# Two-headed attention and gated MLP on one core: a second copy of one head's queries and keys, and a later start of DMA transposes

## The chip, the cores and the metric

The kernel runs on one core of a Trainium2 chip. A core has a matmul engine (TensorE, here PE, with PEld for its weight loads), a vector engine (DVE), a scalar engine (ACT), a general engine (GpSimd, here POOL) and a sync engine (SP). Each takes its instructions in a written order, and they wait for each other on semaphores. POOL and SP issue DMAs; 16 DMA engines carry them. The metric is the time on the device in microseconds (us), the median of several executions.

## The reference

Four batches, eight heads, 768 positions, 64 features a head. Heads 0, 2 and 6 ("retrieval") attend to all earlier positions; heads 1, 3, 4, 5 and 7 ("streaming") to the first 4 positions and the last 64. The attention output goes token by token through a gated MLP with a residual:

```python
scores = np.matmul(q, k.transpose(0, 1, 3, 2)) / np.sqrt(D)
full_mask = causal                                   # heads 0, 2, 6
stream_mask = causal & (is_sink | in_win)            # the others
a = softmax(where(mask, scores, -1e9))
x = np.matmul(a, v)            # heads side by side: 3072 tokens x 512
h = gelu(x @ w_gate) * (x @ w_val)                   # 512 -> 1536
out = x + sigmoid(x @ w_res) * (h @ w_out)           # 1536 -> 512
```

## The kernel before

**Chunks.** The 3072 tokens are done in six chunks of 512, four tiles of 128 positions each. Chunk 0 is tiles 0 to 3 of batch 0, chunk 1 tiles 4, 5 of batch 0 and 0, 1 of batch 1, chunk 2 tiles 2 to 5 of batch 1; chunks 3 to 5 do the same for batches 2 and 3. For each chunk there is an attention stage and then a gate/value stage (`gate_value`, 48 matmuls of 512 columns with `wg` and 48 with `wv`, L1076; in chunk 0 partly in halves of 256 columns, L1058). The output stage (`output`: `wr` at L1106, `wo` at L1121) of a chunk is spread over the attention stage of the next one.

**Head pairs.** Heads go in pairs: (0, 2), (4, 6), (1, 3), (5, 7), numbered 0 to 3. The tile `qkt` holds, for each pair, the transposed queries and keys: the first head of a pair on partitions 0 to 63, the second on 64 to 127. A score matmul (L817) reads 64 partitions, so the two heads of a pair use the two row halves of PE. `attention` fills 512-column banks of PSUM with score blocks: first a bank with the diagonal blocks of each head, then, for a retrieval head alone, banks with the blocks below the diagonal. `scores` takes two banks at a time. In pair (4, 6) head 4 is streaming and head 6 is retrieval, so all banks after the first are head 6's. ACT takes the exponentials (L833), DVE masks the diagonal ones (L869), PE weighs the values (L941, L951, and L965 for the first four positions), DVE normalises (L995, L1006, L1008).

**Transposes.** The chunk's attention output must be transposed into `xT` before the gate matmuls. `to_features` does it with 8 matmuls against the identity per two pairs (L1030) and an eviction by ACT or DVE (L1037). `to_features_dma` does it with one DMA transpose issued on SP (L1021). From chunk `DT_FIRST` on, the pair that comes second in the chunk's order uses the DMA. That constant also sets the order of the pairs in a chunk: `ORDER` = 0, 2, 1, 3 before it, `LATER` = 1, 3, 0, 2 from it on.

**Loads.** POOL issues all loads from HBM, which turn 32-bit into 16-bit values on the way: queries and keys into one of two staging buffers `qks`, values into `va`, and the weights. Chunks 0 and 1 load queries and keys in rows (`loads_rows`) and transpose them on PE (L672). From chunk 2 on `loads_natural` transposes them from `qks` into `qkt` by DMA on SP, eight per four-tile segment (`dT`, L710). SP also issues the shifted copies of values (`vs`, L632) and the output stores (L1132, from five buffers `otile`). SP takes these strictly in order.

**What sets the order.** All work is recorded as tasks with a duration, dependencies and a priority. `Graph.schedule` plays a planned run and from it writes a fixed order for each engine; a task's `late` is added to a DMA's planned arrival. `HINTS` overrides the priorities of single tasks by number. Matmuls on the blank tile (L1138) keep PE busy until the first gate matmul; their number also comes from the plan.

Of the kernel before, what the change touches and what calls it, by code (L numbers as in the profile page):

```python
# [5 lines left out]
SEQ = 768  # L6
# [12 lines left out]
FP16 = mybir.dt.float16  # L19
# [17 lines left out]

LATER = (1, 3, 0, 2)
ROWS_UNTIL = 2
DT_FIRST = 2  # L40
DT_ALL = 9

VK = ((1, 4), (3, 4), (4, 5), (4, 7))


HINTS = (
    "0:39.65 1:493.12 14:469.96 398:-242.8 399:-201.03 400:-217.49 401:-77.67 405:543.9 410:-3184.9 "
    "583:533.02 585:-204.99 599:508.01 644:14.56 655:-31.08 656:-70.92 657:-3147.66 663:547.65 679:533.02 "
    "686:474.28 687:-25.49 690:1.7 691:-170.24 693:-141.72 694:-39.96 695:-202.5 698:53.9 702:20.38 "
    "706:-3046.83 710:493.09 711:169.94 714:-171.05 715:-2884.34 720:380.6 726:-201.02 727:493.29 "  # L50
    "728:-180.62 729:1551.24 732:478.51 735:2337.32 738:-2942.11 739:33.9 740:-81.33 741:-73.37 744:493.83 "
    "745:-3105.95 746:-1850.78 747:566.96 750:296.88 751:114.75 756:-3044 757:-179.11 773:1511.7 835:1504.98 "
    "874:2454.47 910:2410.34 928:2550.33 932:-2014.38 935:3337.35 944:3512.34 958:3480.32 977:2492.95 "
    "979:2505.99 986:2024.82 1004:2016.72 1018:3447.87 1021:3516.2 1091:3558.56 1092:2520.7 1095:2497.83 "
    "1107:1487.53 1136:4457.15 1151:4475.19 1164:4470.56 1236:4527.03 1254:4453.5 1282:2509 1285:4462.07 "
    "1307:5498.98 1311:5603.11 1322:5459.76 1338:5489.56 1355:4132.83 1367:5513.39 1378:4117.99 1463:6535.49 "
    "1475:1955.41 1479:6517.49 1486:6664.6 1494:6511.63 1496:5462.34 1507:6567.8 1512:6315.58 1514:5485.28 "
    "1519:5499.23 1539:5001.96 1559:6315.57 1587:6466.65 1590:6499 1633:7417.82 1638:7410.03 1639:7408.47 "
    "1665:7430.01 1682:6353.3 1684:5484.94 ~632:477.39 ~635:510 "
)  # L60

class Task:
# [40 lines left out]
class Pool:  # L103
# [7 lines left out]
    def can(self, kind, t):  # L111
        if kind in self.caps:
            h = self.held.get(kind, [])
            h[:] = [f for f in h if f is None or f > t]
            if len(h) >= self.caps[kind]:
                return False
        return any(f <= t for f, _ in self.free)
# [341 lines left out]
def build_kernel(nc, q, k, v, w_gate, w_val, w_out, w_res, out):  # L459
    assert N_SINK <= 64 and WINDOW == 64  # L460
    G = Graph(nc)
    sb = lambda name, shape, dt: nc.alloc_sbuf_tensor(name, list(shape), dt)
    many = lambda name, n, shape, dt: [sb(f"{name}{i}", shape, dt) for i in range(n)]
# [13 lines left out]
    P_vs = Pool(many("vs", 2, [128, NT - 1, NHEAD, DHEAD + 1], FP16))  # L477
    P_vk = Pool(many("vk", 2, [128, 8, DHEAD + 1], FP16))
    P_qkt = Pool(many("qkt", 2, [128, 2, NPAIR, SEQ], FP16))
    P_er = Pool(many("er", 2, [128, 4608], FP16))  # L480
    P_es = Pool(many("es", 2, [128, 1024], FP16))
    P_ek = Pool(many("ek", 1, [128, 640], FP16))
# [16 lines left out]
    def at(buf):  # L499
        if buf.pool is P_ps:  # L500
            return psum[:, buf.slot[0] * 512:(buf.slot[-1] + 1) * 512]
        return buf.pool.items[buf.slot]
# [73 lines left out]
    def batch(b):  # L576
        if b not in batches:
            B_ = B()
            B_.v, B_.vs, B_.vk, B_.qkt = Buf(P_v), Buf(P_vs), Buf(P_vk), Buf(P_qkt)
            B_.vtok, B_.vstok, B_.qtok, B_.ktok = {}, {}, {}, {}  # L580
            batches[b] = B_
        return batches[b]

# [112 lines left out]
    def loads_natural(c, si, b, a, z):  # L696

        n = z - a
        BB = batch(b)
        st = Buf(P_st)  # L700
        base = -15 if c == 1 else 1000 * (c - 2) + 50
        for i in range(a, z):
            for j, src in ((1, k), (0, q)):
                def sv(i=i, j=j):
                    return at(st)[:, (j * 4 + i - a) * 512:(j * 4 + i - a + 1) * 512]
                ds = [dma("pool", base, 0.45,
                          (lambda sv=sv, o=o: lambda: sv().rearrange("p (o h d) -> p o h d", o=2, h=4)[:, o, :, :])(),
                          src[b, :, i * 128:(i + 1) * 128, :].rearrange("(h o) p d -> o p h d", o=2)[o], bufs=[st],
                          grp=("ld", b, i, j)) for o in range(2)]
                t = G.add("sp", 1.65, (lambda sv=sv, i=i, j=j: lambda e: e.dma_start(  # L710
                    at(BB.qkt)[:, j, :, i * 128:(i + 1) * 128], sv(), transpose=True))(), ds, base, bufs=[st, BB.qkt], dma=0.6, name="dT")
                for p in range(NPAIR):
                    (BB.ktok if j else BB.qtok)[p, i] = t
            if i == a:
                values(b, a, z, base, False)

    phase = {}

# [3 lines left out]
    def attention(c, segs, xbuf, xtbuf, xtoks, xttoks, l0=0, last=(), ek=None):  # L722
        tiles = [(b, i) for (b, a, z) in segs for i in range(a, z)]

        base = 1000 * c - (200 if len(tiles) < 4 and not l0 else 0)
        n0 = len(ph(c, "sc"))
        todo = []
        order = ORDER if c < DT_FIRST else LATER
        for k_, p in enumerate(order):
            P = B()  # L730
            P.heads, P.p, P.c, P.pr = PAIRS[p], p, c, base + 40 * k_
            retr = [IS_RETRIEVAL[h] for h in P.heads]


            banks = []
            for x in range(2):
                mine = [[(b, i if retr[x] else None, i, 1) for b, i in tiles]]
                rest = [(b, kt, max(a, kt + 1), z - max(a, kt + 1)) for b, a, z in segs for kt in range(z - 1)] if retr[x] else []
                for r in sorted(rest, key=lambda r: -r[3]):
                    for bk in mine:  # L740
                        if sum(y[3] for y in bk) + r[3] <= 4:
                            bk.append(r)
                            break
                    else:
                        mine.append([r])
                banks += [(g, x, bk) for g, bk in enumerate(mine)]
            size = lambda t: sum(y[3] for y in t[2])
            banks.sort(key=lambda t: (t[0], -size(t), t[1]))
            P.et = Buf(P_er if any(retr) else P_es)
            P.where, P.ready = {}, {}  # L750
            P.off = 0
            for g in range(0, len(banks), 2):
                scores(P, tiles, [t[1:] for t in banks[g:g + 2]], g, retr)
            todo.append(P)
        sinks = sink_scores(c, [t for t in tiles if t[1] > 0], base + 40 + 5, ek, 256 if l0 else 0)
        for t in ph(c, "sc")[n0:-1]:
# [3 lines left out]
        sc = ph(c, "sc")[:-1]  # L760
# [27 lines left out]
    def scores(P, tiles, banks, g, retr):  # L788
        scr = Buf(P_ps, "sc" if len(banks) > 1 or P.c else "scr")
        deps, mms = [], []  # L790
        lanes = [0.0, 0.0]
        p, pr = P.p, P.pr
        width = [sum(y[3] for y in blocks) * 128 for _, blocks in banks]
        base = [P.off, P.off + width[0]]
        for bi, (x, blocks) in enumerate(banks):
            o, w_ = bi * 512, base[bi]
            half = slice(64 * x, 64 * x + 64)
            for (b, kt, q0, nq) in blocks:
                BB = batch(b)
                deps += [BB.qtok[p, i] for i in range(q0, q0 + nq)]  # L800
                if kt is None:
                    deps += [BB.ktok[p, q0]] + ([BB.ktok[p, q0 - 1]] if q0 else [])
                    parts = [(max(0, q0 * 128 - 64 + 64 * s), q0 * 128 + 64 * s, 64, o + 64 * s) for s in range(2)]
                else:
                    deps.append(BB.ktok[p, kt])
                    parts = [(kt * 128, q0 * 128, nq * 128, o)]
                for i in range(nq):
                    P.where[x, kt, b, q0 + i] = w_ + i * 128
                for (k0, qq, w, oo) in parts:
                    mms.append((lanes[x], len(mms), BB, half, k0, qq, w, oo))  # L810
                    lanes[x] += max(w / 2400, 0.03)
                o += nq * 128
                w_ += nq * 128
        mms.sort(key=lambda m: m[0:2])

        def sc(e):
            return [e.matmul(at(scr)[:, oo:oo + w], lhsT=at(BB.qkt)[half, 1, p, k0:k0 + 128],  # L817
                             rhs=at(BB.qkt)[half, 0, p, qq:qq + w], start=True, stop=True)
                    for (_, _, BB, half, k0, qq, w, oo) in mms]
        qkts = [batch(b).qkt for b in dict.fromkeys(b for b, _ in tiles)]  # L820
        ts = G.add("pe", max(lanes), sc, deps, pr, bufs=[scr] + qkts, name=f"sc{p}")
        ts.mode = "row"
        ph(P.c, "sc").append(ts)

# [14 lines left out]
                    func=AF.Exp, scale=SM_SCALE))(), [ts], pr, bufs=[scr, P.et], fset="exp", name=f"exp{p}"))  # L839
        ph(P.c, "exp").extend(txs)  # L840
        P.off += cols
        for bi, (x, blocks) in enumerate(banks):
            for (b, kt, q0, nq) in blocks:
                for i in range(nq):
                    P.ready[x, kt, b, q0 + i] = txs[bi]
        if g:
            return

        st = {x: base[bi] for bi, (x, _) in enumerate(banks)}
        n = len(tiles)  # L850
        for xs in ([(0, 1)] if retr[0] == retr[1] else [(0,), (1,)]):
            w, L = n * 128, len(xs)
# [385 lines left out]
```

## Time and profile before

| | |
|---|---|
| Time, median of 5 runs | 274.71 us (273.07 to 276.88) |
| The profiled execution's own time | 274.8 us |
| its span, first to last instruction | 273.1 us |
| Matmuls in it | 2392 |
| DVE, ACT busy | 51% of the span each |
| DMA packets, bytes | 96842, 28.86 MB |
| DMA engines busy | 90% or more of each slice up to about 137 us, then little |

The profile is of one execution. In its rows "start us, us" stand first, then engine, line, operation, out<-in, how many in a row; what stands in brackets is idle time of the engine just before and what ended it. Rows of a table by stretch give the stretch, its length and the busy time of PE, PEld, DVE, ACT and POOL (or without a column where an engine has none), then the granted clock of PE, the DMA engines' share and GB/s. A row of a DMA issue ends with the us from its issue to its landing. Matmul durations in rows include the pipeline's depth, so what a matmul costs is read from one start to the next.

### The profile page before, as it was taken

How to read it: one execution, taken by the hardware profiler on the slowest of the kernel's cores; microseconds unless marked ns; L12 is line 12 of the kernel's file. 1: busy time of each engine (PE TensorE's matmuls, PEld its weight loads, DVE VectorE, ACT ScalarE, POOL GpSimd, SP SyncE). 2: the span in 40 equal slices, each digit the busy share in tenths (PEclk: the TensorE clock that was granted, in tenths of full speed). 3: DMA queues.
4: the chain of work that ended last, by engine and by line, in shares of the span. 5: the costliest groups of instructions: out<-in, count | busy, mean ns of one | idle time of the engine just before them, and what ended most of it. 6: DMA issues, size and time to landing. Idle time of an engine off the chain costs nothing.

```text
span 273.1 us, 5673 instructions
## 1 busy us (share of the span) xinstructions
PE 265.8 (97%) x2392; PEld 139.4 (51%) x2392; DVE 139.8 (51%) x271; ACT 140.6 (51%) x217; POOL 87.1 (32%) x124
## 2 busy tenths in 40 slices
PE   7999999999999999799999999999999999999995
PEld 6768455465444455344455444455444455544444
DVE  1698135477335286335466534467643357643444
ACT  2776437785425876143775143787232878244210
POOL 8999405996908009993000000000000000000000
PEclk9999999999999999999999999999999999999999
DMA  6999999999999999999954200013200015010013
GB/s 87 168 201 207 184 180 229 164 154 156 164 172 149 159 113 230 155 175 177 149 138 80 77 0 0 2 41 79 79 0 0 0 41 79 21 59 1 0 38 118
DMA packets 96842, 28.86 MB, mean 106 GB/s; under 512 B 85424, under 2 KB 93232, under 8 KB 96816
## 3 DMA queue, kind: packets, MB, share of 16 engines
q0 software_dynamic: 70320, 14.69, 63.5%
q1 hardware_dynamic: 26496, 13.80, 28.6%
q8 instruction: 19, 0.31, 0.5%
q14 instruction: 7, 0.06, 0.1%
HBM read 29.36 MB, written 6.29 MB: 131 GB/s over the span
## 4 chain that ended last, share of the span: by engine, by line
PE 85%; DMA 8%; POOL 4%; issue 1%; DVE 1%; POOLq 0%; DVEq 0%
PE ps L1076 42%; PE ps L1121 22%; PE ps L1106 8%; DMA wg<-in_moe_w_gate_dram 5%; PE ps L817 5%; DMA xT<-x 3%; PE ps L951 3%; PE ps L941 2%; PE ps L965 1%; PE ps L1058 1%; POOL qks L551 1%; POOL va L551 1%; PE ps L1030 1%; PE ps L672 1%; PE ps L908 1%
## 5 line engine op out<-in xcount | busy, mean ns | idle before, releaser
L1090 DVE SCALAR_TENSOR_TENSOR hT<-gact,ps 128x512 f16<-128x512 f16 x68 | 46.0, 686 | 68.4 <-ACT gact L1088 57.0
L1088 ACT ACTIVATE gact<-ps 128x512 f16<-128x512 f32 x68 | 39.8, 597 | 77.9 <-PE ps L1076 77.5
L1076 PE MATMUL ps<-xT,wg 128*128 128x512 f16 x272 | 75.7, 379 | 2.3 <-DMA xT<-x 1.7
L1076 PE MATMUL ps<-xT,wv 128*128 128x512 f16 x272 | 75.4, 379 | 0.0
L1121 PE MATMUL ps<-wo,hT 128*128 128x512 f16 (+2 forms) x312 | 70.7, 363 | 0.0
L1076 PEld LDWEIGHTS ps<-xT,wg 128*128 128x128 f16 x272 | 26.3, 98 | 33.8 <-DMA xT<-x 2.2
L1076 PEld LDWEIGHTS ps<-xT,wv 128*128 128x128 f16 x272 | 26.3, 98 | 31.0 <-DVE hT L1090 0.4
L1121 PEld LDWEIGHTS ps<-wo,hT 128*128 128x128 f16 x312 | 27.2, 98 | 25.5 <-issue 0.6
L833 ACT ACTIVATE er<-ps 128x1024 f16<-128x1024 f32 (+4 forms) x40 | 34.2, 891 | 10.3 <-PE ps L817 10.0
L551 POOL DMA_DIRECT2D qks<-in_k_dram x36 | 28.3, 826 | 34.2 <-DMA qkt<-qks 20.6
L551 POOL DMA_DIRECT2D qks<-in_q_dram x36 | 28.8, 844 | 0.8 <-POOLq L1220 0.8
L1125 DVE SCALAR_TENSOR_TENSOR otile<-srs,ps 128x512 f32<-128x512 f32 (+2 forms) x26 | 16.6, 644 | 18.7 <-PE ps L1121 16.2
L1106 PE MATMUL ps<-wr,xT 128*128 128x512 f16 x96 | 24.7, 380 | 0.0
L551 POOL DMA_DIRECT2D va<-in_v_dram x24 | 21.4, 946 | 2.5 <-PE ps L965 2.5
L1109 ACT ACTIVATE srs<-ps 128x512 f32<-128x512 f32 x24 | 14.4, 598 | 11.2 <-PE ps L1106 10.9
L817 PE MATMUL ps<-qkt 64*128 64x64 f16 (+3 forms) x399 | 17.9, 215 | 0.0
L1008 DVE TENSOR_TENSOR xtok<-ps,rcp 128x512 f32<-128x512 f32 (+1 forms) x28 | 16.9, 608 | 0.5
L1128 DVE TENSOR_TENSOR otile<-otile,xtok 128x512 f32<-128x512 f32 (+2 forms) x26 | 16.7, 648 | 0.6
L817 PEld LDWEIGHTS ps<-qkt 64*128 64x128 f16 x399 | 10.3, 94 | 8.8 <-issue 4.2
L1106 PEld LDWEIGHTS ps<-wr,xT 128*128 128x128 f16 x96 | 8.7, 98 | 10.7 <-issue 1.2
L1138 PE MATMUL ps<-blank 128*128 128x128 f16 x117 | 11.8, 253 | 2.0 <-DVE blank L523 2.0
L833 ACT ACTIVATE es<-ps 128x1024 f16<-128x1024 f32 (+1 forms) x14 | 12.6, 899 | 1.4 <-PE ps L817 1.4
(67 smaller groups left out, 211.6 us busy)
## 6 DMA issues: line engine op xcount, KB each, us to landing
out_dram<-otile SPq DMA_DIRECT2D x23, 256.0 KB, 2.4
va<-in_v_dram POOLq DMA_DIRECT2D x24, 128.0 KB, 18.5
qks<-in_k_dram POOLq DMA_DIRECT2D x32, 64.0 KB, 9.8
qks<-in_q_dram POOLq DMA_DIRECT2D x32, 64.0 KB, 10.0
wg<-in_moe_w_gate_dram POOLq DMA_DIRECT2D x3, 512.0 KB, 11.6
wv<-in_moe_w_val_dram POOLq DMA_DIRECT2D x3, 512.0 KB, 11.9
wo<-in_moe_w_out_dram POOLq DMA_DIRECT2D x4, 384.0 KB, 25.0
vs<-va SPq DMA_DIRECT2D x4, 260.0 KB, 6.1
```

What stands on the lines that cost most here:

```text
L551: return G.add(eng, issue, lambda e: e.dma_start(out_ap(), in_ap), deps, prio, bufs=bufs, dma=cost, name=name, grp=grp)
L817: return [e.matmul(at(scr)[:, oo:oo + w], lhsT=at(BB.qkt)[half, 1, p, k0:k0 + 128], rhs=at(BB.qkt)[half, 0, p, qq:qq + w], start=True, sto ...
L833: return e.activation(out=o, in_=i_, func=AF.Exp, scale=SM_SCALE)
L1008: t2 = G.add("dve", c_dve(2 * n * 64), lambda e: e.tensor_tensor(out=xview(), in0=avv(0, DHEAD), in1=scale(), op=ALU.mult), [t1] + xdeps, ...
L1076: return lambda e: [e.matmul(at(dst)[:, :], lhsT=w[:, ci, f * 128:(f + 1) * 128], rhs=at(xtbuf)[:, ci, :], start=(ci == 0), stop=(ci == NC ...
L1088: ta = G.add("act", c_act(512), (lambda gb=gb, ga=ga: lambda e: e.activation(out=at(ga)[:, :], in_=at(gb)[:, :], func=AF.Gelu))(), [tg], p ...
L1090: th = G.add("dve", c_dve(512), (lambda vb=vb, ga=ga, f=f: lambda e: e.scalar_tensor_tensor(out=at(h)[:, f, :], in0=at(ga)[:, :], scalar=0 ...
L1106: e.matmul(at(rb)[:, :], lhsT=at(xtbuf)[:, ci, s], rhs=wr[:, ci, :], start=(ci == 0), stop=(ci == NCB - 1))
L1109: ta = G.add("act", c_act(512), (lambda rb=rb, sr=sr: lambda e: e.activation(out=at(sr)[:, :], in_=at(rb)[:, :], func=AF.Tanh, scale=0.5)) ...
L1121: e.matmul(at(fb)[:, w], lhsT=at(h)[:, fi, s], rhs=wo[:, fi, w], start=(fi == 0), stop=(fi == NF - 1))
L1125: t1 = G.add("dve", c_dve(n), (lambda fb=fb, sr=sr, ot=ot, w=w: lambda e: e.scalar_tensor_tensor(out=at(ot)[:, w], in0=at(sr)[:, w], scala ...
L1128: t2 = G.add("dve", c_dve(n), (lambda ot=ot, lt=lt, w=w: lambda e: e.tensor_tensor(out=at(ot)[:, w], in0=at(ot)[:, w], in1=at(xbuf)[:, lt, ...
```

## The change

For chunks 2 to 5 the transposed queries and keys of head 6, which lie on partitions 64 to 127 of `qkt`, are also copied to partitions 0 to 63 of a new tile `q6`: one DMA on SP for each loaded segment, five in all. In pair (4, 6) the banks below the diagonal are then paired: one computed in the upper row half from `qkt` and one in the lower from `q6`. Banks that need tiles without a copy (tiles 0 and 1 of batch 1) stay in the upper half. `DT_FIRST` goes from 2 to 3, so chunk 2 transposes all of its attention output on PE and takes its pairs in the order 0, 2, 1, 3. The planned arrival of the key and query transposes is 3 us later and that of the copies 2 us. `HINTS` is replaced as a whole, so the written order of every engine differs.

```diff
-DT_FIRST = 2
+DT_FIRST = 3
...
 HINTS = (
...
+    P_q6 = Pool(many("q6", 2, [128, 2, SEQ], FP16))
...
+            B_.q6, B_.q6tok = None, {}
...
+        if BB.q6 is None:
+            BB.q6 = Buf(P_q6)
+        loaded = []
         for i in range(a, z):
             for j, src in ((1, k), (0, q)):
...
                 t = G.add("sp", 1.65, (lambda sv=sv, i=i, j=j: lambda e: e.dma_start(
                     at(BB.qkt)[:, j, :, i * 128:(i + 1) * 128], sv(), transpose=True))(), ds, base, bufs=[st, BB.qkt], dma=0.6, name="dT")
+                t.late = 3.0
+                loaded.append(t)
...
+        t = G.add("sp", 0.8, lambda e: e.dma_start(at(BB.q6)[0:64, :, a * 128:z * 128], at(BB.qkt)[64:128, :, 1, a * 128:z * 128]),
+                  loaded, base + 1, bufs=[BB.qkt, BB.q6], dma=0.4, name="q6")
+        t.late = 2.0
+        for i in range(a, z):
+            BB.q6tok[0, i] = BB.q6tok[1, i] = t
...
+                if p == 1 and x == 1:
+                    can = lambda bk: all((0, i) in batch(b).q6tok and (1, kt) in batch(b).q6tok
+                                         for b, kt, q0, nq in bk for i in range(q0, q0 + nq))
+                    left, mine = sorted(mine[1:], key=lambda bk: -sum(y[3] for y in bk)), mine[:1]
+                    low = [bk for bk in left if can(bk)]
+                    up = [bk for bk in left if not can(bk)]
+                    while up or low:
+                        mine.append((up or low).pop(0))
+                        if low or up:
+                            lower.append(id(low[0])) if low else None
+                            mine.append((low or up).pop(0))
...
-            half = slice(64 * x, 64 * x + 64)
+            lane = 0 if low else x
+            half = slice(64 * lane, 64 * lane + 64)
...
+                if low:
+                    q6s.add(BB.q6)
+                    deps += [BB.q6tok[0, i] for i in range(q0, q0 + nq)] + [BB.q6tok[1, kt]]
...
-            return [e.matmul(at(scr)[:, oo:oo + w], lhsT=at(BB.qkt)[half, 1, p, k0:k0 + 128],
-                             rhs=at(BB.qkt)[half, 0, p, qq:qq + w], start=True, stop=True)
-                    for (_, _, BB, half, k0, qq, w, oo) in mms]
+            side = lambda BB, low, j: at(BB.q6)[:, j, :] if low else at(BB.qkt)[:, j, p, :]
+            return [e.matmul(at(scr)[:, oo:oo + w], lhsT=side(BB, low, 1)[half, k0:k0 + 128],
+                             rhs=side(BB, low, 0)[half, qq:qq + w], start=True, stop=True)
+                    for (_, _, BB, half, k0, qq, w, oo, low) in mms]
```

## The prediction

> **What bounds the kernel now.** I read the page first: its busy shares, then the chain of waits, then a table of busy time by stretch whose cuts are the starts and ends of the gate/value phases, and last the timeline of the matmul engine at the few places where the table leaves idle time.
>
> ```profile
> PE 265.8 (97%) x2392; PEld 139.4 (51%) x2392; DVE 139.8 (51%) x271; ACT 140.6 (51%) x217; POOL 87.1 (32%) x124
> ...
> PE 85%; DMA 8%; POOL 4%; issue 1%; DVE 1%; POOLq 0%; DVEq 0%
> ...
> 88.20:106.50 18.30, 18.30 (x229) 9.52 (x227) 11.19 (x24) 15.53 (x21) 4.74 (x8) 1.00 1.78 155
> 106.50:114.40 7.90, 6.17 (x51) 2.99 (x44) 3.72 (x7) 0.99 (x2) 7.77 (x12) 1.00 1.70 184
> 114.40:132.60 18.20, 18.20 (x86) 8.11 (x88) 7.94 (x13) 7.31 (x14) 10.85 (x14) 1.00 2.05 172
> ```
>
> TensorE (PE) is busy in every microsecond from 28.5 us to the last matmul, except in the row 106.50:114.40, where 6.17 of 7.90 us are busy. So two things count: what PE streams, and the few places where it stands. The clock column is 1.00, so a streamed column has one price. In the timeline, 128x512 matmuls start 0.216 us apart (10 of them from 28.53 to 30.70), 128-column transposes 0.056 us apart. The two places where PE stands:
>
> ```profile
> 111.58 1.03 PE L1076 MATMUL ps<-xT,wv 128*128 128x512 f16 x4
> 114.34 0.60 PE L1076 MATMUL ps<-xT,wg 128*128 128x512 f16 x2 [1.73 <-DMA xT<-x]
> ...
> 27.40 0.59 PE L1076 MATMUL ps<-xT,wg 128*128 128x512 f16 x2
> 28.53 2.33 PE L1076 MATMUL ps<-xT,wg 128*128 128x512 f16 x10 [0.54 <-DMA wg<-in_moe_w_gate_dram]
> ```
>
> Start to start, the first lost 114.34-111.58-4x0.216 = 1.90 us, the second 28.53-27.40-2x0.216 = 0.70. The first is the DMA transpose of chunk 2's attention output. It takes 7.8 us to land there; chunk 3's, issued at 144.12 when the loads are done, takes 3.8.
>
> ```profile
> xT<-x SPq DMA_TRANSPOSE x1, 7.8
> ...
> vs<-va SPq DMA_DIRECT2D x1, 260.0 KB, 9.1
> ```
>
> **Head 6 in both row halves.** Scores are 64-row matmuls; two heads run side by side. In pair (4, 6) head 4 has 4 diagonal blocks and head 6 its diagonal plus all earlier key tiles, so one half works while the other waits:
>
> ```profile
> 90.59 0.83 PE L817 MATMUL ps<-qkt 64*128 64x64 f16 x14
> 91.35 0.39 PE L1106 MATMUL ps<-wr,xT 128*128 128x512 f16 x1
> ...
> 98.96 0.61 PE L817 MATMUL ps<-qkt 64*128 64x128 f16 x10
> 99.51 0.22 PE L941 MATMUL ps<-vs,es 128*64 128x65 f16 x1
> ```
>
> The group of 14 streams 2048 columns (1536 in head 6's half, 512 in the other) and holds PE for 91.35-90.59 = 0.76 us; the group of 10, pair (0, 2), also streams 2048, 1024 a half, and holds it for 0.55. There are six lopsided groups in chunks 2 to 5: 0.76 and 0.66 (93.43 to 94.09), 0.66 (132.57), 0.77 (172.82), 0.76 and 0.67 (216.72, 219.56). In the changed program's order each has an equal or nearly equal share in both halves (chunk 2 too, where key tiles 0 and 1 have no copy but are paired with tiles that have one). At 0.55 each: -0.21-0.11-0.11-0.22-0.21-0.12 = **-0.98 us**. The number of score matmuls (399) stays.
>
> The copy itself is five small DMAs on SP's queue. Each waits until the key and query transposes of its segment have landed, and SP stands meanwhile. Behind the first stand five of chunk 3's transposes; behind the later ones chunk 1's and 2's output stores, the shifted value copies and chunk 3's output transpose. The last transpose of chunk 2's segment is issued at 72.82 and takes 9.2 us, so the first copy issues near 82. No row shows this copy; the nearest is the 260 KB SBUF copy above, issued at 74.15, 9.1 us. The Trainium skill, "DMA: Bandwidth & Descriptors", section "Anatomy of one DMA", puts one DMA at a fixed 2.0 us plus its bytes over 436 GB/s[...]. By the row it lands at 91. In the new order pair (4, 6) is third in chunk 2, some 8 us after the 90.6 start, near 98: covered[...] by the row with 7. I take the row and price the copy at 0; each us beyond 7 would be a us of PE. What it holds back on SP (under 1.5 us a time by the gaps between transposes) is covered too: chunk 3's keys are all issued by 94.4 and land by about 102, and are first read at 132.57; the stores wait on five output buffers, and the next one is wanted after 132; chunk 3's output transpose issues at 144.12, the queue's last key transpose at 135.8, some 5 us of margin. GpSimd issues the same loads, only with staging buffers swapped.
>
> **Output transposes of chunk 2 on PE.** Gone is the 1.90 us stall. In its place come 8 more transposes (64 to 72 in the program), 8 x 0.056 = +0.45 us, and two evictions (424 ns on DVE or 592 on ACT, both under half busy in that stretch). The change also puts pairs (0, 2), (4, 6) first in chunk 2. Tile-mode changes on PE go from 121 to 122; one costs 0.095 us (the last 512-column matmul before a score group, 90.28, to the group's 90.59 is 0.31, not 0.216). +0.10. Behind the last values of the chunk the chain is reciprocal 206 ns, normalising 690, transposes 450, eviction about 600: 1.95 us. The new order puts 2 gate and 4 output matmuls ahead of those transposes (6 x 0.216 = 1.3 us) and 4 output and 4 gate/value ones behind (1.7 us), against 0.9 of normalising and 0.6 of eviction. Without that cover up to 1 us would show. Chunk 1 has this same form now and PE does not stand there. So **-1.90+0.55**.
>
> **The start.** The planned arrival times and the reordered hints issue nothing themselves but move everything. The first matmul on the third gate block comes after 8.1 us of PE work counted from the first gate matmul (21.06 us), before after 6.8, so its load, landed at 28.5, no longer stops PE: -0.70. But chunk 1's key transposes move from 42.05 to after 15.4 us of that work, 36.6 us; their last load does not land before 36.8:
>
> ```profile
> 42.05 1.53 PE L672 MATMUL ps<-ident,qks 128*64 128x128 f16 x48
> ...
> qks<-in_k_dram POOLq DMA_DIRECT2D x1, 256.0 KB, 18.0
> ```
>
> (issued at 18.83). +0.3 with the wake-up. When the first gate matmul runs is unknown within half a us: both orders have the same attention work ahead of it, the new one 8 fewer idle matmuls. This load caps what an earlier start could bring. **-0.40.**
>
> **The sum:** -0.98+0.45+0.10-1.90-0.70+0.30 = -2.7 us. The profiled execution took 274.8 us (span 273.1 and 1.7 around it), the median is 274.71: 272.1 against the execution, 272.0 against the median.
>
> **The rivals.**
> *A wait in place of the removed one (0.20).* Chunk 2's end, or another seam in a fully new order on PE: the engines run in a written order, and every plan has places where data is some tenths late. For it: PE has no slack, so each is paid. Against: all other seams of the present order lose 0.1 to 0.3 us each. If 0.4 is lost in each of four chunks: 272.0+1.6 = 273.6.
> *Halves that don't overlap on two tiles (0.06).* The copy lives in another SBUF tile. Then the 0.98 stays: 273.0. Against: two heads of one tile on different partitions do overlap at 0.55.
> *Slower: output weights starved by earlier loads (0.10).* Freeing the staging buffer 4 us earlier lets GpSimd issue chunk 2's loads from 40 us and not 43.99, while the four blocks of the output weights are still on their way (issued 23.9 to 26.1, 23.3 to 26.8 us to land, the last at 52.9); PE wants the last at 53 us. If loads and weights shared the engines evenly from 45 on, the 7.6 us of weights left would take 15, the last landing at 60 and PE standing 7 us: 279. It decides from about 3 us of lateness. The same skill page, "Queues, rings and completion order", says an engine takes turns between queue rows, packet by packet: that would be this case if loads and weights were on two rows. Both are issued by GpSimd and fall under the one software queue of the page's list, and in the trace the loads issued from 43.99 land 10 us later, after the weights, whose landings stay 1.9 us apart. By the trace it costs 0; the rule's end stays in the chance.
>
> **How the numbers follow.** Forecast 0.58, its own range 270.9 to 273.0 (half a us of start either way, the tenths at seams, and the scatter of the five runs, 273.1 to 276.9, of which the median keeps little). A better case, 0.06: the new order loses less at its seams than the 1.2 us that the present one loses apart from the stalls named above; all of it gone gives 270.8. Rivals 0.20, 0.06 and 0.10. A measurement of this kernel can tell about 1% from no change; 1% faster is 271.96, which lies at the forecast's middle, so I put 0.32 of its 0.58 below: faster 0.32+0.06 = 0.38; same 0.26+0.20+0.06, less 0.01 = 0.51; slower 0.11, the slow rival and that 0.01. The range of 8 in 10 leaves the slow rival out and half of the ends: 270.5 to 274.5.
>
> **What would show it.** Right: no wait on the output transpose in chunk 2; six score groups at 0.55; one short wait on a load near 36.7 us; the last matmul 2 to 3 us sooner. Wrong: a wait of PE on the copy or on output weights, idle tenths at each seam, or chunk 2's stretch before its gate phase as long as before.

## The result and the profile after

| | before | after |
|---|---|---|
| Median | 273.03 us of 80 runs | 272.25 us of 43 runs |
| Lowest to highest | 271.65 to 278.07 | 270.99 to 272.84 |
| Quarter and three-quarter marks | 272.3 and 274.4 | 271.5 and 272.4 |
| Profiled execution, time and span | 274.80 and 273.1 | 272.46 and 270.6 |

The ratio after to before is 0.9957, with an interval of 0.9942 to 0.9971: a gain of 0.4%, about 1.2 us by the ratio and 0.8 by the medians. The forecast was 272.0 us, so the time is right to 0.25 us. The gain is not: 2.7 us was forecast. The two profiled executions do differ by 2.5 us in span, but 65 of before's 80 runs were quicker than its profiled one. The table shows a second effect that the forecast did not have: the changed kernel has lost the upper tail. Its highest run lies below the median of before. The changed kernel's 43 runs lie in two groups, 20 from 270.99 to 271.89 us and 23 from 272.12 to 272.84; both of its profiles fell in the upper one, and what separates the groups is open.

From the page of the changed kernel, the busy times and the chain of work that ended last:

```profile
PE 264.5 (98%) x2392; PEld 139.4 (51%) x2392; DVE 141.5 (52%) x275; ACT 139.8 (52%) x215; POOL 86.9 (32%) x124
...
PE 94%; DVE 4%; issue 1%; DVEq 0%
```

PE was busy for 265.8 us and is now for 264.5. The 8% of the chain that belonged to DMA is gone. The table by stretch of the changed kernel, for the attention stage of chunk 2 and the gate/value stage behind it:

```profile
88.00:107.90 19.90, 19.90 (x241) 10.59 (x239) 11.36 (x22) 15.79 (x21) 7.07 (x10) 1.00 1.82 174
107.90:127.00 19.10, 19.10 (x117) 9.10 (x110) 9.44 (x17) 5.92 (x11) 15.99 (x21) 1.00 2.06 173
```

PE is busy in all of it, where before 1.73 us were missing ahead of 114.34. The view of what PE waits for, changed kernel (total, times, longest):

```profile
PE ps L1173 <- DVE blank L525: 2.6, 1, 2.6
PE ps L852 <- DVE xT L1072: 0.3, 1, 0.3
```

The first is the start of the program and the second lies at 19.8 us, among the matmuls on the blank tile. From there to the end none is listed.

The timeline of PE in the changed kernel, at the two score groups of pair (4, 6) in chunk 2:

```profile
98.24 0.61 PE L852 MATMUL ps<-qkt 64*128 64x64 f16 x13
98.48 0.38 PE L852 MATMUL ps<-q 64*128 64x384 f16 x2
98.80 1.04 PE L1141 MATMUL ps<-wr,xT 128*128 128x512 f16 x4
...
101.06 0.39 PE L852 MATMUL ps<-qkt 64*128 64x512 f16 x1
101.06 0.28 PE L852 MATMUL ps<-q 64*128 64x256 f16 x1
101.18 0.50 PE L852 MATMUL ps<-qkt 64*128 64x64 f16 x16
101.61 0.22 PE L976 MATMUL ps<-vs,es 128*64 128x65 f16 x1
```

The operand `q` is the copy in the lower row half; at 101.06 one matmul from the copy and one from `qkt` start together. From the group's start to the next operation are 0.56 and 0.55 us, as forecast, against 0.76 and 0.66 before. The four later groups take 0.55 (130.44), 0.56 (173.89), 0.55 (211.80) and 0.55 (216.73).

### The profile page after: what moved, and what is told of

It reads as the page before. It is cut to its first block, busy times and chain, and to the rows that moved or that the text cites. A ratio compares the mean times of both kernels' runs of the same rounds, so it can differ in the third digit from the quotient of the medians.

```text
span 270.6 us, 5686 instructions
## 1 busy us (share of the span) xinstructions
PE 264.5 (98%) x2392; PEld 139.4 (51%) x2392; DVE 141.5 (52%) x275; ACT 139.8 (52%) x215; POOL 86.9 (32%) x124
## 4 chain that ended last, share of the span: by engine, by line
PE 94%; DVE 4%; issue 1%; DVEq 0%
PE ps L1111 44%; PE ps L1156 23%; PE ps L1141 8%; PE ps L852 5%; PE ps L986 3%; PE ps L1093 3%; PE ps L1173 2%; PE ps L976 2%; PE ps L676 2%; PE ps L1000 2%; PE ps L1065 1%; DVE vs L620 1%; PE ps L943 1%; DVE er L904 0%; DVE es L904 0%
## 5 line engine op out<-in xcount | busy, mean ns | idle before, releaser
L1111 PE MATMUL ps<-xT,wv 128*128 128x512 f16 x272 | 74.6, 379 | 0.0
L1111 PE MATMUL ps<-xT,wg 128*128 128x512 f16 x272 | 74.1, 379 | 0.0
L852 PE MATMUL ps<-qkt 64*128 64x64 f16 (+3 forms) x391 | 16.9, 213 | 0.3 <-DVE xT L1072 0.3
L1173 PE MATMUL ps<-blank 128*128 128x128 f16 x109 | 11.1, 254 | 2.6 <-DVE blank L525 2.6
```

The lines of the kernel that those rows point to most:

```text
L852: return [e.matmul(at(scr)[:, oo:oo + w], lhsT=side(BB, low, 1)[half, k0:k0 + 128], rhs=side(BB, low, 0)[half, qq:qq + w], start=True, sto ...
L1111: return lambda e: [e.matmul(at(dst)[:, :], lhsT=w[:, ci, f * 128:(f + 1) * 128], rhs=at(xtbuf)[:, ci, :], start=(ci == 0), stop=(ci == NC ...
L1173: G.add("pe", 0.06, lambda e, warm=warm: e.matmul(at(warm)[:, 0:128], lhsT=blank[:, :], rhs=blank[:, :], start=True, stop=True), [t_blank] ...
```

## The experiments

Two theories were open after the result. The first: before's profiled execution had an unusually long stall on the output transpose, and the usual one is short, so removing it brings little. The second: some part of the change costs time that the profile hides, as the copies on SP or the eight more transposes might.

**Before, unchanged, three more times.** The first was timed in 12 executions, the other two in one each.

> The kernel before once more, unchanged, for a second profile. Theory A: the wait of TensorE on chunk 2's output transpose (1.90 us in the first profile, taken in an execution of 274.8 us, while the median of many is 273.0) differs from execution to execution with the state of the loads, and is nearer to 0.5 to 1.2 us in a middling one. Theory B: the wait is fixed at about 1.9 us, and what is missing from the forecast gain was lost in the new order. Ratio 1.00 either way; the profile decides: under A the wait is clearly shorter than 1.9 us in an execution of 273 us or less, and the weights' landing at the start moves too.

> The kernel before, a third profile. Two profiles so far fell on executions of 274.8 and 274.1 us and show a wait of 1.9 and 1.25 us on chunk 2's output transpose, while half of the executions take under 273. Theory A: time and wait go together: an execution near 272 shows under 0.4 us of it. Theory B: the wait is always above 1.2 us.

> The kernel before, a fourth profile, for the same question as the run before it: under theory A the execution's time less the wait of TensorE on the output transpose and on the first weights is nearly the same in all four (near 272), under theory B it is not.

The kernel against itself gave 273.89 and 273.09 us, ratio 1.0025 (0.9991 to 1.0059). Read from start to start, as in the prediction, the four profiles of this one program lose:

| Time of the execution | at the third gate block | output transpose issued, landed | lost on it | time less both losses |
|---|---|---|---|---|
| 274.80 | 0.70 | 106.52, 114.29 | 1.89 | 272.2 |
| 274.11 | 0.30 | 104.51, 113.46 | 1.23 | 272.6 |
| 272.88 | 0 | 102.57, 112.34 | 0.68 | 272.2 |
| 272.43 | 0 | 102.33, 111.78 | 0.07 | 272.4 |

The last column is constant within 0.4 us: the two stalls account for what separates these four executions of before. The timeline of SP's queue shows where the difference starts, first in the 274.80 execution:

```profile
97.24 5.97 SPq L710 DMA_TRANSPOSE qkt<-qks  x4
103.25 1.23 SPq L632 DMA_DIRECT2D vs<-va  x2
104.52 1.95 SPq L1132 DMA_DIRECT2D out_dram<-otile  x2
106.52 1.94 SPq L1021 DMA_TRANSPOSE xT<-x  x1
```

and the same queue in the 272.43 execution:

```profile
94.95 4.90 SPq L710 DMA_TRANSPOSE qkt<-qks  x3
99.89 1.23 SPq L632 DMA_DIRECT2D vs<-va  x2
101.17 1.12 SPq L1132 DMA_DIRECT2D out_dram<-otile  x2
102.33 2.83 SPq L1021 DMA_TRANSPOSE xT<-x  x1
```

The operations and their order are the same. Key and query transposes that wait for loads end about 3.4 us apart (103.21 and 99.85), and everything behind them, the output transpose too, moves with them. Why the loads come at different times is open. In the quick execution PE goes through almost without a break. Its timeline:

```profile
110.89 1.03 PE L1076 MATMUL ps<-xT,wv 128*128 128x512 f16 x4
111.82 0.60 PE L1076 MATMUL ps<-xT,wg 128*128 128x512 f16 x2
```

Four matmuls at 0.216 us end at 111.75, the transpose landed at 111.78, and PE lost 0.07 us. So the first theory holds: the usual stall is shorter than the one first profiled.

**The changed kernel, all of head 6 in one half.** The copies are made, but no score reads them.

```diff
-            half = slice(64 * lane, 64 * lane + 64)
+            half = slice(64 * x, 64 * x + 64)
...
-            side = lambda BB, low, j: at(BB.q6)[:, j, :] if low else at(BB.qkt)[:, j, p, :]
+            side = lambda BB, low, j: at(BB.qkt)[:, j, p, :]
```

> The changed kernel with every engine's order and all copies kept, but head 6's banks below the diagonal all computed in the upper row half from the original tile. If TensorE has no slack and the two halves overlap on two tiles as they do on one, this loses the whole term of 0.98 us: 0.9 to 1.0 us slower than the changed kernel, so near 273.2 and within 0.1 us of the kernel before. If the halves do not overlap across two tiles, or the time is lost again at the next wait, it is as fast as the changed kernel (272.2).

It took 272.89 us (272.27 to 273.44), ratio to before 0.9972 (0.9938 to 1.0005). Its timeline of PE at the same two groups:

```profile
97.92 0.83 PE L852 MATMUL ps<-qkt 64*128 64x64 f16 x15
98.69 1.04 PE L1141 MATMUL ps<-wr,xT 128*128 128x512 f16 x4
...
100.95 0.73 PE L852 MATMUL ps<-qkt 64*128 64x512 f16 x18
101.61 0.22 PE L976 MATMUL ps<-vs,es 128*64 128x65 f16 x1
```

The groups take 0.77 and 0.66 us again.

**The same without the copies**, beside the changed kernel itself on one chip:

```diff
-        t = G.add("sp", 0.8, lambda e: e.dma_start(at(BB.q6)[0:64, :, a * 128:z * 128], at(BB.qkt)[64:128, :, 1, a * 128:z * 128]),
-                  loaded, base + 1, bufs=[BB.qkt, BB.q6], dma=0.4, name="q6")
-        t.late = 2.0
...
-            half = slice(64 * lane, 64 * lane + 64)
+            half = slice(64 * x, 64 * x + 64)
```

> The changed kernel without the five copies and with all of head 6's banks in the upper row half, as in the run one_half; SP has five DMAs fewer, TensorE's order is kept. If the copies are hidden, as the forecast had it, this is as fast as one_half (0.6 to 1.0 us slower than the changed kernel). If they cost time on SP or in the DMA engines, it is faster than that by their price.

> The changed kernel once more, on the chip of the other runs of this set: 272.2, 0.3 to 0.6% under the kernel before, with a narrow scatter; in its profile no wait on an output transpose in chunk 2.

Without copies it took 272.91 us (272.35 to 273.50), and the changed kernel 272.01 (271.08 to 272.65; ratio to before 0.9971, 0.9941 to 1.0001, so this repeat by itself can't tell the gain from none). The difference of the two, 0.90 us, is what both halves bring, less what the copies cost. The kernel with copies and one half (272.89) ran on another chip, where before had a median of 273.09 and not 272.38; its time alone doesn't price the copies. The profiles do, because the three kernels share the order of PE: the time from the first key transposes of chunk 1 to the last group of output matmuls can be compared. For the changed kernel in its two profiles, the transposes start at 36.83 and 36.74 (rows in the next section) and the last group here:

```profile
264.91 2.81 PE L1156 MATMUL ps<-wo,hT 128*128 128x256 f16 x36
...
264.81 2.81 PE L1156 MATMUL ps<-wo,hT 128*128 128x256 f16 x36
```

With copies and one half, and below it without copies:

```profile
36.51 0.64 PE L676 MATMUL ps<-ident,qks 128*64 128x128 f16 x16 [0.31 <-DMA qks<-in_k_dram]
265.55 2.81 PE L1156 MATMUL ps<-wo,hT 128*128 128x256 f16 x36
...
36.88 0.64 PE L679 MATMUL ps<-ident,qks 128*64 128x128 f16 x16
265.92 2.81 PE L1156 MATMUL ps<-wo,hT 128*128 128x256 f16 x36
```

That is 228.08 and 228.07 us with both halves, 229.04 with copies and one half, and 229.04 without copies. So the five copies cost nothing in the changed order, against the second theory, and reading head 6 in both halves brings 0.97 us.

**Before, with chunk 2's output transposed on PE, and nothing else.** Priorities go by task name here and wherever else the list of tasks differs, so that the tasks kept keep theirs.

```diff
-                if c >= DT_FIRST and P.p == order[1]:
+                if c >= 3 and P.p == order[1]:
```

> The kernel before with chunk 2's DMA transpose replaced by eight transposes on TensorE, the pairs' order and all planned priorities kept. Costs 0.45 us of streaming and gives back the wait on the DMA. Theory A: the middling wait is 0.5 to 1.2 us, so 0 to 0.7 us faster than the kernel before, and the executions scatter less upwards. Theory B: 1.9-0.5, so 1.4 us faster.

It took 273.51 us (272.59 to 274.83) against 273.09, ratio 1.0029 (1.0002 to 1.0056). No wait on `xT` is left in its profile, yet it isn't quicker. Eight transposes take 0.45 us (102.52 to 102.97), and where PE passes from one kind of work to the next behind chunk 2 it now loses 0.18 us (ahead of 136.46) and 0.19 us (ahead of 143.39): 0.82 in all. What it saves is the stall, which in a middling execution of before is about as long. Against the four times less both losses (272.2 to 272.6) it is 0.9 to 1.3 us slower.

**The copies and both halves, with chunk 2's output transpose left to DMA.** Priorities are those of before, and the planned arrivals of the key and query transposes are not moved. Against the changed kernel:

```diff
-DT_FIRST = 3
+DT_FIRST = 2
...
-                t.late = 3.0
```

> The kernel before with the copy of head 6 and the two row halves alone: DMA transposes from chunk 2 on, pair (4, 6) second in the order 1, 3, 0, 2 as before, no later planned arrivals, the priorities of before. Saves up to 0.98 us of streaming. If that reaches the end, about 1 us faster than the kernel before; the wait on chunk 2's output transpose stays and may grow by what TensorE arrives earlier (0.3 us in chunk 2), so 0.6 to 1.0 us. If the saving only lengthens that wait or another one, no difference.

It took 281.29 us (280.77 to 283.83), ratio 1.0319 (1.0261 to 1.0378). SP's queue shows the reason:

```profile
106.77 0.46 SPq L637 DMA_DIRECT2D vs<-va  x1
109.95 0.62 SPq L725 DMA_DIRECT2D q<-qkt  x1
110.61 0.59 SPq L1167 DMA_DIRECT2D out_dram<-otile  x1
111.25 1.37 SPq L1056 DMA_TRANSPOSE xT<-x  x1
```

SP stood from 107.23 to 109.95 on a copy whose transposes landed at 109.87. A store and the output transpose were behind it, and the transpose landed at 116.01, when PE had long been waiting:

```profile
PE ps L1111 <- DMA xT<-x: 3.7, 1, 3.7
...
PE ps L1065 <- DVE x L1041: 1.4, 2, 1.1
PE ps L1111 <- DVE xT L1072: 1.2, 2, 0.6
PE ps L1111 <- DMA wg<-in_moe_w_gate_dram: 0.7, 1, 0.7
```

These waits sum to 7.0 us. Together with 1.7 us of a slower clock (last section), less 0.9 for the two halves, they give 280.2 from the 272.4 without stalls; the profiled execution took 280.99.

**The same with the planned arrival 3 us later** (`t.late = 3.0` kept). PE's order of matmuls is the same as in the kernel above; on SP the copy now comes behind the output transpose.

> The run rows_alone (head 6's copy and two row halves, the rest as before) with one thing added: the key and query transposes are planned to land 3 us later. TensorE's order is the same, matmul for matmul; on SP the third copy now stands behind chunk 2's output transpose and not ahead of it. Theory C: the 8 us that rows_alone lost came from that copy, which stood on SP until 109.95 us waiting for key transposes to land and held back the output transpose behind it (issued at 111.25, in the kernel before at 106.5); then this kernel gets 4 to 7 us of them back, 274 to 277. Theory D: they came from the changed order on TensorE (output matmuls used up too early); then it stays at 280 to 281.

It took 278.11 us (275.79 to 279.41), ratio 1.0185 (1.0128 to 1.0241), between the ranges of the two theories. The transpose is issued at 104.12, not 111.25, but takes 9.5 us to land, and PE still waits 2.2 us on it. So the copy's place on SP explains about 3 of the 8 us. For the rest, the waits in this profile are the 2.2 us on the landing, 2.6 us on DVE and 0.7 us on a load at the start. Those on DVE are the same in both kernels, 0.26 and 0.61 us in chunk 2 and 1.12 and 0.61 in the last chunk: PE's new order comes too early to the output transposes and the gate matmuls there. With 1.7 us of a slower clock, less 0.9 for the two halves, they give 278.7 from 272.4; the profiled execution took 278.58. How far the 2.2 us come from PE's new order and how far from the long landing was not settled.

**The changed kernel, with chunk 2's pair (1, 3) transposed by DMA again.**

```diff
-                if c >= DT_FIRST and P.p == order[1]:
+                if c >= 2 and P.p == order[1]:
```

> The changed kernel with chunk 2's pair (1, 3), second in its order, transposed by DMA again, its eight TensorE transposes and two evictions gone. On SP the DMA stands ahead of chunk 2's copies that wait. It streams 0.45 us less. Between its issue and the gate matmul that needs it there are some 6 us of TensorE work, and the same DMA took 7.8 us to land in the first profile of before. If it lands in time: 0.45 us faster than the changed kernel (271.8); if it takes 7 to 8 us: 0.5 to 1.5 us slower with wide scatter (272.7 to 273.7).

It took 283.91 us (283.13 to 284.79), ratio 1.0412 (1.0368 to 1.0456). Its chain of waits:

```profile
101.65 0.69 DVE x L1044
...
109.29 7.80 DMA xT<-x
117.10 0.05 issue
117.14 21.40 PE ps L1114 x86
```

The pair's values were ready at 102.34. SP issued their transpose at 109.29, because two key transposes that wait for loads stand ahead of it, and it landed at 117.10. PE waited 8.28 us on it, where the expectation was a kernel at most 1.5 us slower. In the changed order, then, this DMA transpose costs 12 us.

**Before, with the loads held back.** From 102 us on, GpSimd's loads wait until chunk 2's output transpose has landed.

```diff
+    xd = next(t for t in G.tasks if t.name == "xD")
+    held = next(t for t in G.prog["pool"] if t.grp is not None and t.grp[:3] == ("ld", 3, 0))
+    held.waits = held.waits + [xd]
```

> The kernel before with one more wait on GpSimd: the loads that it issues from 102 us on wait until chunk 2's output transpose has landed; every order is kept. If the transpose lands late because it shares the DMA engines with these loads, it lands within 4 to 5 us of its issue, TensorE does not wait for it in chunk 2, and the executions above 274 us become rare; the loads then end some 9 us later, with up to 1 us at chunk 3's output transpose, which stands behind their transposes on SP. If it lands late for its own work or for the transposes on SP ahead of it, it still takes 7 to 9 us.

The transpose landed 5.2 us after its issue at 101.61, against 7.8 to 9.8 with the loads running, and PE did not wait on it. So the long landing comes from the loads, or from the key and query transposes that follow them on SP and were held back with them; which of the two was not separated. The kernel was slower all the same: 276.83 us (274.76 to 278.10), ratio 1.0147 (1.0092 to 1.0202). The held loads were wanted. DVE's timeline in its quickest execution:

```profile
127.14 1.05 DVE L597 COPY vk<-va 4x130 f16<-4x130 f16 x2 [3.88 <-DMA va<-in_v_dram]
```

DVE stood for 3.88 us on a small copy of late values; the products `hT` of the gate stage were queued behind it, and PE waited 3.0 us on `hT`. Four of its six executions add a slower clock to that (last section).

No experiment gave a kernel quicker than the changed one.

## Why the prediction was right and wrong

**The time was right because the base was.** The 274.80 execution less its two stalls is 272.2 us, which the other three executions confirm (272.2 to 272.6). From there the forecast took 0.98 for the two halves and added 0.55 for the transposes and 0.30 for the load at the start: 272.1. Measured are 272.25 and, on one chip alone, 272.01. That the forecast from the median came out as well is luck: the median of the five runs stood 1.7 us above that of 80, and the forecast gain was too large by nearly as much.

**The gain was wrong in two terms of its sum,** the stall of 1.90 and the 0.70 on the third gate block. Both were read correctly, but from one execution, and taken as properties of the kernel. Over four executions they are 0.07 to 1.89 and 0 to 0.70, and the median of 80 runs, 273.03, lies 0.7 us above the 272.35 that is the mean of the last column. So about 0.7 us was there to win in the middle, not 2.6. The five runs shown hid this, since their median of 274.71 matched the profiled execution. The step that failed is the one that sets the profiled execution against the median, finds them equal and so takes both stalls, -1.90 and -0.70, as gain in full.

**Both halves: right.** Forecast 0.98 us; measured 0.96 over the six groups (4.28 us in one half, 3.32 in both), 0.97 over the stretch from the key transposes to the last matmuls, and 0.90 in the medians. The rival that two tiles would not overlap is refuted by the 0.55 us groups.

**The copy at nothing: right, but only in this order.** The first copy was issued at 77.82 us (forecast near 82), landed 8.4 us later and was first read at 98.48. The five landed in 2.5 to 8.4 us, median 6.1, all under the row taken (9.1). The section of the Trainium skill that the forecast names there ("DMA: Bandwidth & Descriptors", "Anatomy of one DMA — SWDGE (gpsimd) path") fits its figure to DMAs that GpSimd issues; these copies are issued by SP, so it gives none for them. The forecast asked what the copies hold back on SP and named chunk 3's output transpose, with 5 us of margin. It did not say that chunk 2's would have been held back as well, had it stayed there: the kernel with copies and both halves alone is 8 us slower, some 3 of them by this. The parts were summed as if each could stand by itself.

**Transposes on PE: right in price, misplaced in purpose.** The transposes take the forecast 0.45 us; the 0.10 for one more mode change was not seen by itself. The version with this part alone pays 0.37 us more where PE's work changes over; in the changed kernel's own order PE waits nowhere near chunk 2. In the median this part pays about what it saves. It takes away the upper tail: the highest run falls from 277.00 to 274.83 with this part alone, and from 278.07 to 272.84 with the whole change. And it takes the output transpose off the queue on which the copies wait. One sentence there names pairs (0, 2) and (4, 6) as the first of chunk 2; the order is (0, 2), (1, 3), (4, 6), (5, 7), as the sentence on the copies has it. No number hangs on it.

**The start: the cap was right, but not alone.** The two profiled executions of the changed kernel start their first gate matmul at 21.30 and 19.73 us, yet end their last matmul at 267.72 and 267.62. The timeline of PE in the later-started one:

```profile
36.83 0.64 PE L676 MATMUL ps<-ident,qks 128*64 128x128 f16 x16
37.40 1.90 PE L1111 MATMUL ps<-xT,wg 128*128 128x512 f16 x8
```

and in the earlier one:

```profile
35.61 0.60 PE L1093 MATMUL ps<-xT,wv 128*128 128x256 f16 x4
36.74 0.64 PE L676 MATMUL ps<-ident,qks 128*64 128x128 f16 x16 [0.53 <-DMA qks<-in_k_dram]
37.31 1.90 PE L1111 MATMUL ps<-xT,wg 128*128 128x512 f16 x8
```

The lead of 1.57 us is down to 0.69 just ahead of the key transposes and to 0.09 at them. So their load, forecast to cap the start near 36.7 us, does, and takes 0.60 us of the lead. The other 0.88 went to two blocks of the gate and value weights, on which the earlier execution waits (idle 0.34 us ahead of 28.30 and 0.20 ahead of 30.84): the stall that the forecast counted as gone for 0.70 us comes back when PE starts sooner. The wait on the key load that was forecast shows only in the earlier one.

**The rivals.** In chunk 2 and behind it no wait took the place of the removed one. The slow rival did not come: the output weights landed from 44.8 to 50.4 us, earlier than before (52.9) and ahead of PE's need, although the loads behind them were issued from 40.73.

## What to carry to other kernels

A stall that ends on a DMA is a sample, not a property of the kernel: profile the same program a few times before you count the stall as gain, and subtract the stalls from each execution's time to find the base that does not move. On a queue taken strictly in order, a small transfer that costs nothing by itself delays whatever is issued behind it by the time that its own inputs are late, so look behind it for a transfer that the critical engine wants. Parts of a change that share such a queue can't be priced one by one: here one part alone cost 8 us, another gained nothing, and together they gained 0.8 us by the medians, 1.2 by the ratio.

## What the runs showed of the hardware

A stall on PE can cost more than its length. The table by stretch of the kernel with later planned arrivals (its column before the last two is the granted clock):

```profile
113.60:118.00 4.40, 4.38 (x13) 1.72 (x14) 0.69 (x1) 0.60 (x1) 4.40 (x7) 0.61 1.71 189
118.00:134.40 16.40, 16.40 (x77) 7.26 (x76) 7.26 (x12) 6.69 (x13) 4.93 (x7) 1.00 1.95 173
```

and its timeline of PE at the end of the wait:

```profile
113.62 0.66 PE L1112 MATMUL ps<-xT,wg 128*128 128x512 f16 x2 [2.24 <-DMA xT<-x]
114.06 1.06 PE L1112 MATMUL ps<-xT,wv 128*128 128x512 f16 x2
114.92 1.06 PE L1112 MATMUL ps<-xT,wg 128*128 128x512 f16 x2
...
117.47 0.60 PE L1112 MATMUL ps<-xT,wv 128*128 128x512 f16 x2
```

Two matmuls take 0.86 us from start to start where they took 0.43: half the clock for about 3.4 us. Ten matmuls from 113.62 to 117.47 take 3.85 us instead of 2.16, so the stall cost 1.7 us more than its length. Of this kernel's six executions, three at a mean clock of 1.00 took 275.8, 276.0 and 277.6 us, and three at 0.994 took 278.6 to 279.4. The 3.69 us stall of the kernel with copies and both halves alone cost the same 1.7 us extra (ten matmuls in 3.86 us, from 116.05 to 119.91). With the 8.28 us stall the extra was 2.7 us (14 matmuls in 5.71 us, from 117.14 to 122.85). The 1.73 us stall of before and the 2.96 us of the kernel with held loads left the pace at 0.43 in their profiles; of the latter's six executions that profile was the quickest, and four show a mean clock of 0.994 (276.8 to 278.1 us, against 274.8 and 275.3 at 1.00). The Trainium skill, "TensorE: Matmul & The Clock Gate", section "HAM oscillation — how this bites in real kernels", names idle gaps of over about 3.4 us as the ones that bring the clock down. Here a gap of 2.24 us did it, with 0.61 and 0.26 us of idle time shortly ahead of it (3.1 us idle in the 5.6 us to 113.62), and one of 2.96 us did not: in these traces the single gap's length doesn't decide. What does was not settled.
